# A gated causal convolution without padding columns in its token ring: shorter older taps and one product per run

## The chip, the cores and the metric

The kernel runs on one core of a Trainium2 chip. The metric is device time in microseconds (us) of one execution. Engines in the profile: PE is TensorE's matmuls, PEld its weight loads, DVE is VectorE, ACT is ScalarE, POOL is GpSimd, SP issues nearly all transfers. Times in ns are single instructions.

## The reference

Attention in blocks of 64 over 8 batches, 8 heads, 576 tokens, 64 numbers per head; its output is turned into x (8 x 576 x 512) and goes through a gated layer with a causal depthwise convolution of five taps:

```
scores = q @ k^T / 8, where block(i) >= block(j);   attn = softmax(scores) @ v
x   = attn, heads side by side                        # B x 576 x 512
xp  = 4 zero tokens ahead of each batch of x
gate_pre[s] = sum over k=0..4 of conv_w[k] * xp[s + k] # per channel
out = (sigmoid(gate_pre) * (x @ w_val)) @ w_out
```

Tap k = 4 is the token itself; tap k < 4 is the token 4-k back. A batch's first tokens have no older ones: there the reference reads zeros.

## The kernel before, in words

The whole order of work is written out by hand: PLAN (lines 12 to 116) is a list of words such as `C/1/P/4+5+6+7`, that is step, arguments, engine (P is PE, V DVE, A ACT, G POOL, S SP), PSUM banks. The last lines of the kernel go through it once and call the function of each word; each engine executes its own words in that order and waits only for data and buffers. Eight PSUM banks are shared by all.

**Attention.** `lq`, `lk`, `lv` load on SP; `cd`, `cv` cast to fp16 on POOL or DVE; `Tt` turns q and k on PE and `Te` copies them from PSUM into qkT; `S` computes scores of 128 keys and `E` their exponentials on ACT (pt); `mka`, `mkb` zero masked corners on POOL; `A` multiplies with v, `Nr` and `Nm` divide by the sums on DVE (x16); `X` turns the result on PE, and `Xe` copies it into the ring. The last 64 tokens of a batch go by `SL`, `EL`, `AT`, `NTr`, `NTm`, `XT`, `XTe`. `Sh` and `Eh` are halves of `S` and `E` at the start.

**The token ring.** xt (line 226 on, tile "xt") holds x turned, 128 partitions x 4 channel groups x the tokens of four batches side by side; batch b lies in slot b mod 4. Ahead of each slot, and after the last, lie 4 columns of zeros, which `px` writes once on POOL (lines 335 to 339). So a slot has 580 columns, and the ring 2320 (RING, line 138). `Xe` (line 584) and `XTe` (line 573) write at slot + 4.

**The convolution, the value and the product.** The ring is cut into five runs of 464 columns (RUN); as batches 4 to 7 take the place of 0 to 3, runs 0 to 4 are done a second time as 5 to 9. For run n:

- `C` (line 626): 80 matmuls. Each has a 32x32 diagonal of convolution weights (DG) as its loaded weights and streams 464 columns. For each of five taps it goes over d and over four row groups of 32 partitions (line 633: channel group g = (row + d) mod 4), so that the 16 matmuls of one tap sit on 16 different 32x32 tiles of the array; row decides the PSUM bank, g the 32 output partitions. Tap kk reads the ring at o + kk.
- `CS` (line 639), twice: tanh on ACT of two banks each into th (the sigmoid is 0.5 * (1 + tanh(x/2)); the 0.5 is folded into w_out).
- `V` (line 645), four times: four matmuls of 128x128 weights (w_val) that stream 464 ring columns each.
- `Ve` (line 653), four times: (th + 1) * value on DVE into gv, which has no padding; so it issues one operation for each batch that the run touches, one or two.

`O` (line 673) multiplies 128 tokens of gv with w_out, `Oe` copies to SBUF, `Od` stores. In runs 1, 2 and 3 (and 6, 7, 8) a batch starts inside the run; in 0 and 4 (5 and 9) none does.

Of the kernel before, what the change touches and what calls it, by code (L numbers as in the profile page):

```python
# [26 lines left out]
Nr/0/V A/1/P/2+3 Nm/0/V lwv/1/S E/4.1/A cd/3.1/G S/4.0/P/6+7 Nr/1/V lwv/0/S S/5.2/P/0+1 Nm/1/V  # L27
E/4.0/A lwo/1/S X/0/P/4+5 Tt/3.1/P/4+5 cv/3/G S/4.2/P/2+3 lq/4.1/S Te/3.1/V E/5.2/A mka/3/G
w0/1.128.0/P/6 lq/4.0/S mkb/3/G X/1/P/6+7 mkb/2/G A/3/P/6+7 lk/4.0/S E/4.2/A Xe/0/V lv/4.1/S cv/2/G
S/6.0/P/0+1 Nr/3/V S/5.1/P/4+5 Nm/3/V cvt/0/G E/6.0/A A/2/P/2+3 px//G Xe/1/V mka/4/G X/3/P/2+3  # L30
E/5.1/A S/6.1/P/6+7 mkb/4/G Nr/2/V AT/0/P/0 Nm/2/V E/6.1/A lk/4.1/S Xe/3/V S/5.0/P/4+5 NTr/0/V
X/2/P/2+3 lv/6.0/S w0/1.128.0/P/1 E/5.0/A Xe/2/V mka/6/G S/7.2/P/6+7 NTm/0/V cwv/1/G S/6.2/P/2+3
E/7.2/A C/0/P/0+1+4+5 lv/6.1/S cwv/0/V E/6.2/A cwo/0/V V/0.3/P/6 CS/0.1/A lq/5.0/S cwo/1/G V/0.2/P/7
CS/0.0/A Ve/0.3/V S/7.1/P/4+5 V/0.0/P/2 Ve/0.2/V E/7.1/A lq/5.1/S cd/4.0/G W//P/0+1+6+7 Ve/0.0/V
lv/5.1/S S/7.0/P/4+5 We/1/A We/0/V V/0.1/P/3 lv/5.0/S mkb/6/G cv/4/G lv/7.1/S E/7.0/A Tt/4.0/P/6+7
Ve/0.1/V lv/7.0/S XT/0/P/2 cd/4.1/G A/4/P/0+1 Te/4.0/A lvt/1/S O/0.0/P/3 Nr/4/V Nm/4/V lk/5.0/S
# [83 lines left out]
def kernel(  # L120
# [10 lines left out]
    nc = tc.nc  # L131
    fp32 = mybir.dt.float32
    fp16 = mybir.dt.float16
    AF = mybir.ActivationFunctionType
    ALU = mybir.AluOpType

    B, H, SEQ, D = q.shape
    RING, RUN = 4 * (4 + SEQ), 464
    out2d = out.rearrange("b s n -> (b s) n")

    made = []

    def mm(out, lhsT, rhs, start=True, stop=True):
        made.append(nc.tensor.matmul(out=out, lhsT=lhsT, rhs=rhs, start=start, stop=stop,  # L144
                                     skip_group_check=True))
# [9 lines left out]
    def const(shape, dt, tag):  # L155
        return cpool.tile(shape, dt, tag=tag, name=tag)

    def consts(n, shape, dt, tag):
        return [const(shape, dt, f"{tag}_{i}") for i in range(n)]
# [5 lines left out]
    def one(b):  # L165
        return PS[0:128, b]

    def pick(t, banks):
        a, e = banks
        return t[0:128, a:e + 1:e - a]  # L170

    def both(banks):
        return pick(PS, banks)

    def one16(b):
        return PS16[0:128, b]

    def both16(banks):
        return pick(PS16, banks)
# [3 lines left out]
    def take(*key):  # L183
        taken.append(where.pop(key))
        return taken[-1]
# [12 lines left out]
    def placed(*key):  # L198
        banks, zs = spots.pop(key)
        return take(*key), 256 * zs[0]  # L200
# [5 lines left out]
    w_val_sb = const([128, 4, 512], fp16, "w_val")  # L206
# [3 lines left out]
    DG = const([128, 20, 32], fp16, "DG")  # L210
# [4 lines left out]

    qks = [consts(3, [128, 2, 576], fp32, f"{n}s") for n in "qk"]
    vs = consts(5, [128, 4, 2, 64], fp32, "vs")
    raw = consts(3, [128, 2, 576], fp16, "raw")
    vts = consts(2, [128, 8, 64], fp32, "vts")
    qk16 = [consts(2, [128, 9, 2, 64], fp16, f"{n}16") for n in "qk"]  # L220
    qkT = consts(3, [128, 2, 2, 640], fp16, "qkT")
# [5 lines left out]
    rcts = consts(2, [128, 4, 1], fp32, "rct")  # L227
    x16 = consts(4, [128, 4, 2, 64], fp16, "x16")
    xds = consts(2, [128, 4, 64], fp16, "xd")
    xt = const([128, 4, RING + 4], fp16, "xt")  # L230
    ths = consts(3, [128, 4, RUN], fp32, "th")
    wz = ths[2].rearrange("p f s -> p (f s)")[0:128, 0:256].bitcast(fp16)
    gv = const([128, 16 * SEQ], fp16, "gv")
    w_val_st = gv[0:128, 0:4096].bitcast(fp32).rearrange("p (f n) -> p f n", f=4)
    gv = gv.rearrange("p (f s) -> p f s", f=4)
# [3 lines left out]
    w_out_16 = osb_all[0:128, 2048:3072].bitcast(fp16).rearrange("p (f n) -> p f n", f=4)  # L239

    def slot(b):
        return (4 + SEQ) * (b % 4)

    def rot(tiles, i):
        return tiles[i % len(tiles)]
# [3 lines left out]
    def copy(eng, out, in_):  # L249
        if eng == "A":  # L250
            i = nc.scalar.copy(out=out, in_=in_)  # L251
        else:
            i = (nc.vector if eng == "V" else nc.gpsimd).tensor_copy(out=out, in_=in_)  # L253
        made.append(i)
# [76 lines left out]
    def pv(eng, bank=None):  # L331
        for t in v16s:
            nc.gpsimd.memset(t[0:128, 0:4, 0:2, 64:65], 1.0)

    @op
    def px(eng, bank=None):
        for i in range(4):
            nc.gpsimd.memset(xt[0:128, 0:4, slot(i):slot(i) + 4], 0.0)
        nc.gpsimd.memset(xt[0:128, 0:4, RING:RING + 4], 0.0)

    @op
    def pt(eng, bank=None):
# [228 lines left out]

    @op
    def XTe(b, eng, bank=None):
        copy(eng, xt[0:128, 0:4, slot(b) + 516:slot(b) + 580],
             one16(take("XT", b))[:, 0:256].rearrange("p (g s) -> p g s", g=4))

    @op
# [5 lines left out]
    @op  # L583
    def Xe(p, eng, bank=None):
        b, g = divmod(p, 4)
        bank, o = placed("X", p)
        copy(eng, xt[0:128, g, slot(b) + 4:slot(b) + 516].rearrange("p (i r s) -> p i r s", i=4, r=2),
             both16(bank)[:, :, o:o + 256].rearrange("p r (i s) -> p i r s", i=4))


# [27 lines left out]
    def We(i, eng, bank=None):  # L618
# [3 lines left out]
        else:  # L622
            made.append(nc.vector.tensor_scalar(out=o, in0=r, scalar1=0.5, scalar2=None, op0=ALU.mult))

    @op
    def C(n, eng, bank):
        o = RUN * (n % 5)
        for i in range(2):
            where["C", n, i] = bank[2 * i:2 * i + 2]
        for kk in range(5):  # L630
            for d in range(4):
                for row in range(4):
                    g = (row + d) % 4
                    rs, cs = slice(32 * row, 32 * row + 32), slice(32 * g, 32 * g + 32)
                    mm(one(bank[row])[cs, 0:RUN], DG[rs, 5 * g + kk, 0:32],
                       xt[rs, g, o + kk:o + kk + RUN], start=(kk == 0), stop=(kk == 4))

    @op
    def CS(n, i, eng, bank=None):
        made.append(nc.scalar.activation(  # L640
            out=rot(ths, n)[0:128, 2 * i:2 * i + 2], in_=both(take("C", n, i))[:, :, 0:RUN],
            func=AF.Tanh, bias=0.0, scale=0.5))

    @op
    def V(n, x, eng, bank):
        o = 4 + RUN * (n % 5)
        where["V", n, x] = bank
        for fc in range(4):
            mm(one(bank)[:, 0:RUN], w_val_sb[0:128, fc, 128 * x:128 * x + 128],
               xt[0:128, fc, o:o + RUN], start=(fc == 0), stop=(fc == 3))  # L650

    @op
    def Ve(n, x, eng, bank=None):
        o, r = RUN * (n % 5), one(take("V", n, x))
        for i in range(4):
            a, e = max(o, slot(i)), min(o + RUN, slot(i) + SEQ)
            if a < e:
                made.append(nc.vector.scalar_tensor_tensor(  # L658
                    out=gv[0:128, x, a - 4 * i:e - 4 * i], in0=rot(ths, n)[0:128, x, a - o:e - o],
                    scalar=1.0, in1=r[:, a - o:e - o], op0=ALU.add, op1=ALU.mult))  # L660


    def project(u, t, r, a, e):
# [47 lines left out]
    for word in PLAN.split():  # L711
        name, args, eng, bank = (word.split("/") + [""])[0:4]
        a = [int(i) for i in args.split(".") if i]
# [51 lines left out]
```

## Time and profile before

| what | value |
| --- | --- |
| three timed runs | 176.15, 177.96 (median), 178.81 us |
| the profiled execution's own time | 176.63 us |
| its span in the trace | 174.8 us |
| PE busy | 166.7 us, 95% of the span |
| ACT, DVE, POOL busy | 144.9, 123.8, 71.6 us |
| moved by DMA | 40.38 MB, 231 GB/s on average |
| granted PE clock | 0.997 of full |

The page lists busy time by engine, the span in 40 slices, the chain of work that ended last, and the costliest groups of instructions; each group's row gives line, engine, operation, out<-in, shapes, count, then busy us, mean ns of one, idle time ahead of it. "64x128" is partitions x columns streamed, "32*32" the tile of the array. Busy PE is not PE at its peak, since matmuls are pipelined.

### The profile page before, as it was taken

The numbers are of one execution on the slowest core, as the hardware profiler recorded it, in microseconds if no ns is written. First come the engines' busy times: TensorE is split into PE (matmuls) and PEld (weight loads), VectorE is DVE, ScalarE is ACT, GpSimd is POOL, SyncE is SP. The second block draws the span as 40 slices with busy tenths as digits, with TensorE's granted clock in tenths as the row PEclk, the third lists the DMA queues.
The fourth block names the chain that finished last, engine by engine and source line by source line (L and its number), as shares of the span: only waits on it lengthen the run. The fifth ranks groups of instructions, "written<-read, shape, count | busy, mean of one in ns | idle before, by whom it ended". The sixth has DMA issues, their size and how long they took to land.

```text
span 174.8 us, 8114 instructions
## 1 busy us (share of the span) xinstructions
PE 166.7 (95%) x3498; PEld 100.4 (57%) x3498; DVE 123.8 (71%) x247; ACT 144.9 (83%) x179; POOL 71.6 (41%) x146
## 2 busy tenths in 40 slices
PE   6999899999999997899999999999999999999991
PEld 1556476456656564577546755566656665665540
DVE  2747898888778791999846998976798695545420
ACT  3699999989999999689889679988798878954562
POOL 5122674982552640576533462253646441100000
PEclk9999999999999999999999999999999999999998
DMA  4999999999999999879899989999994031103175
GB/s 139 302 364 290 248 296 391 307 200 281 189 317 272 201 214 362 252 222 308 252 308 198 281 256 260 306 306 242 332 295 124 4 112 72 64 4 120 38 297 210
DMA packets 53694, 40.38 MB, mean 231 GB/s; under 512 B 39701, under 2 KB 39957, under 8 KB 53658
## 3 DMA queue, kind: packets, MB, share of 16 engines
q1 hardware_dynamic: 53514, 39.74, 78.9%
q8 instruction: 27, 0.44, 1.0%
q10 hardware_dynamic: 144, 0.13, 0.2%
q14 instruction: 9, 0.07, 0.2%
HBM read 30.42 MB, written 9.44 MB: 228 GB/s over the span
## 4 chain that ended last, share of the span: by engine, by line
PE 81%; ACT 6%; DVE 5%; issue 4%; DMA 2%; POOL 0%; DVEq 0%; POOLq 0%; ACTq 0%
PE PS L144 72%; PE PS L148 8%; ACT pt L449 3%; DMA ks<-in_k_dram 2%; ACT qkT L251 2%; DVE qkT L253 2%; DVE x L528 1%; DVE gv L658 1%; DVE xt L253 0%; DVE k L253 0%; DVE rc L523 0%; ACT osb L251 0%; POOL pt L499 0%; POOL pt L494 0%; ACT late L251 0%
## 5 line engine op out<-in xcount | busy, mean ns | idle before, releaser
L449 ACT ACTIVATE pt<-PS 128x1024 f16<-128x1024 f32 (+1 forms) x102 | 93.8, 984 | 10.1 <-PE PS L144 8.5
L144 PE MATMUL PS<-qkT 64*128 64x64 f16 (+4 forms) x512 | 40.2, 260 | 0.8 <-DVE qkT L253 0.5
L144 PE MATMUL PS<-w_out,gv 128*128 128x512 f16 (+1 forms) x148 | 35.8, 374 | 0.2 <-DVE x L528 0.2
L144 PE MATMUL PS<-xt,w_val 128*128 128x464 f16 x160 | 35.7, 360 | 0.0
L253 DVE COPY qkT<-PS 128x1152 f16<-128x1152 f16 (+1 forms) x22 | 29.1, 1327 | 7.4 <-PE PS L148 4.1
L658 DVE SCALAR_TENSOR_TENSOR gv<-th,PS 128x112 f16<-128x112 f32 (+4 forms) x64 | 26.2, 449 | 11.4 <-PE PS L144 6.0
L144 PEld LDWEIGHTS <-pt 128*128 128x128 f16 (+1 forms) x960 | 27.9, 102 | 6.2 <-issue 1.5
L144 PE MATMUL PS<-v,pt 128*128 128x65 f16 (+1 forms) x896 | 31.0, 194 | 0.1
L144 PEld LDWEIGHTS <-qkT 64*128 64x128 f16 x512 | 18.0, 97 | 17.9 <-issue 13.6
L640 ACT ACTIVATE th<-PS 128x928 f32<-128x928 f32 x20 | 17.8, 942 | 6.7 <-PE PS L144 6.6
L528 DVE TENSOR_TENSOR x<-PS,rc 128x512 f16<-128x512 f32 x32 | 22.1, 691 | 1.0
L144 PEld LDWEIGHTS <-w_val 128*128 128x128 f16 x160 | 14.0, 98 | 15.2 <-issue 3.6
L499 POOL MEMSET pt<- 64x256 f16 x32 | 10.4, 329 | 28.9 <-ACT pt L449 28.5
L144 PEld LDWEIGHTS <-gv 128*128 128x128 f16 x148 | 12.6, 97 | 13.4 <-issue 2.3
L253 POOL CAST k<-ks 128x1152 f16<-128x1152 f32 x12 | 14.0, 1166 | 12.3 <-DMA ks<-in_k_dram 7.2
L494 POOL MEMSET pt<- 64x256 f16 x32 | 10.2, 322 | 18.4 <-ACT pt L449 15.9
L253 POOL CAST q<-qs 128x1152 f16<-128x1152 f32 x11 | 13.2, 1201 | 10.2 <-DMA qs<-in_q_dram 9.8
L253 POOL CAST v<-vs 128x512 f16<-128x512 f32 x24 | 14.6, 618 | 6.0 <-DMA vs<-in_v_dram 3.9
L253 DVE COPY xt<-PS 128x512 f16<-128x512 f16 (+1 forms) x30 | 11.6, 397 | 4.5 <-ACT th L640 2.3
L251 ACT COPY qkT<-PS 128x1152 f16<-128x1152 f16 (+1 forms) x16 | 14.3, 908 | 0.4 <-PE PS L148 0.3
L251 ACT COPY osb<-PS 128x512 f32<-128x512 f32 x18 | 10.5, 592 | 3.3 <-PE PS L144 3.0
L144 PE MATMUL PS<-xt,DG 32*32 32x464 f16 x800 | 13.1, 358 | 0.1
(57 smaller groups left out, 140.5 us busy)
## 6 DMA issues: line engine op xcount, KB each, us to landing
ks<-in_k_dram SPq DMA_DIRECT2D x32, 288.0 KB, 5.1
qs<-in_q_dram SPq DMA_DIRECT2D x32, 288.0 KB, 5.7
out_dram<-osb SPq DMA_DIRECT2D x35, 256.0 KB, 4.0
vs<-in_v_dram SPq DMA_DIRECT2D x64, 128.0 KB, 4.9
vts<-in_v_dram SPq DMA_DIRECT2D x8, 128.0 KB, 5.7
osb<-in_moe_w_out_dram SPq DMA_DIRECT2D x2, 512.0 KB, 6.1
gv<-in_moe_w_val_dram SPq DMA_DIRECT2D x2, 512.0 KB
out_dram<-late SPq DMA_DIRECT2D x1, 128.0 KB
```

The source lines that it names most:

```text
L144: made.append(nc.tensor.matmul(out=out, lhsT=lhsT, rhs=rhs, start=start, stop=stop, skip_group_check=True))
L148: made.append(nc.tensor.transpose(out=out, in_=in_, identity=identity))
L251: i = nc.scalar.copy(out=out, in_=in_)
L253: i = (nc.vector if eng == "V" else nc.gpsimd).tensor_copy(out=out, in_=in_)
L449: made.append(nc.scalar.activation(out=o, in_=r, func=AF.Exp, bias=0.0, scale=0.125))
L494: nc.gpsimd.memset(rot(pts, p)[64:128, 0:2, 0:1024].rearrange("p h (t s) -> p h t s", t=2)[:, :, :, 0:64], 0.0)
L499: nc.gpsimd.memset(rot(pts, p)[64:128, 0:2, 640:1408].rearrange("p h (t s) -> p h t s", t=2)[:, :, :, 0:64], 0.0)
L528: made.append(nc.vector.tensor_tensor(out=rot(x16, p)[0:128].rearrange("p i h d -> p h i d"), in0=r[:, :, :, 0:64], in1=rot(rcs, p)[0:128] ...
L640: made.append(nc.scalar.activation(out=rot(ths, n)[0:128, 2 * i:2 * i + 2], in_=both(take("C", n, i))[:, :, 0:RUN], func=AF.Tanh, bias=0.0 ...
L658: made.append(nc.vector.scalar_tensor_tensor(out=gv[0:128, x, a - 4 * i:e - 4 * i], in0=rot(ths, n)[0:128, x, a - o:e - o], scalar=1.0, in ...
```

## The change

The ring loses its padding: slots of 576 columns, 2304 in all, and no `px`. The run edges are written out: 0, 460, 920, 1382, 1842, 2304, so runs have 460 or 462 columns. Tap 4 goes first and streams the whole run, opening the sums in its banks. The older taps leave out the first 4-kk tokens of a batch: where a batch starts inside the run, the new function `tap` returns two pieces, one up to the start and one from start + (4-kk) on, and the loop issues the four row groups of the first piece and then those of the second, for each d. With the batch starts at 576, 1152 and 1728, run 1 is cut into 116 and 344 columns, run 2 into 232 and 230, run 3 into 346 and 114 (less the columns left out of the second piece); run 0 has one piece with its start moved. `Ve` issues one operation for a run. All other words of PLAN stay as they are and where they are.

```diff
-    RING, RUN = 4 * (4 + SEQ), 464
+    RING, EDGES = 4 * SEQ, (0, 460, 920, 1382, 1842, 2304)
...
-    xt = const([128, 4, RING + 4], fp16, "xt")
-    ths = consts(3, [128, 4, RUN], fp32, "th")
+    xt = const([128, 4, RING], fp16, "xt")
+    ths = consts(3, [128, 4, 462], fp32, "th")
...
     def slot(b):
-        return (4 + SEQ) * (b % 4)
+        return SEQ * (b % 4)
+
+    def run(n):
+        return EDGES[n % 5], EDGES[n % 5 + 1]
...
-    def px(eng, bank=None):
-        for i in range(4):
-            nc.gpsimd.memset(xt[0:128, 0:4, slot(i):slot(i) + 4], 0.0)
-        nc.gpsimd.memset(xt[0:128, 0:4, RING:RING + 4], 0.0)
...
+    def tap(o, e, back):
+        starts = [s for s in range(0, RING, SEQ) if o <= s < e]
+        cuts = [o] + [s for s in starts if s > o] + [e]
+        return [(a + back * (a in starts), z) for a, z in zip(cuts, cuts[1:])]
...
     def C(n, eng, bank):
-        o = RUN * (n % 5)
+        o, e = run(n)
...
-        for kk in range(5):
+        for kk in (4, 0, 1, 2, 3):
             for d in range(4):
-                for row in range(4):
-                    g = (row + d) % 4
...
-                    mm(one(bank[row])[cs, 0:RUN], DG[rs, 5 * g + kk, 0:32],
-                       xt[rs, g, o + kk:o + kk + RUN], start=(kk == 0), stop=(kk == 4))
+                for a, z in tap(o, e, 4 - kk) if kk < 4 else [(o, e)]:
+                    for row in range(4):
+                        g = (row + d) % 4
...
+                        mm(one(bank[row])[cs, a - o:z - o], DG[rs, 5 * g + kk, 0:32],
+                           xt[rs, g, a + kk - 4:z + kk - 4], start=(kk == 4), stop=(kk == 3))
...
     def Ve(n, x, eng, bank=None):
-        o, r = RUN * (n % 5), one(take("V", n, x))
-        for i in range(4):
-            a, e = max(o, slot(i)), min(o + RUN, slot(i) + SEQ)
-            if a < e:
-                made.append(nc.vector.scalar_tensor_tensor(
-                    out=gv[0:128, x, a - 4 * i:e - 4 * i], in0=rot(ths, n)[0:128, x, a - o:e - o],
-                    scalar=1.0, in1=r[:, a - o:e - o], op0=ALU.add, op1=ALU.mult))
+        o, e = run(n)
+        made.append(nc.vector.scalar_tensor_tensor(
+            out=gv[0:128, x, o:e], in0=rot(ths, n)[0:128, x, 0:e - o], scalar=1.0,
+            in1=one(take("V", n, x))[:, 0:e - o], op0=ALU.add, op1=ALU.mult))
```

## The prediction, made before the changed kernel ran

> **What bounds the kernel now.** I read the page first: busy times, the 40 slices, the chain of work that ended last, and the groups by shape.
>
> ```profile
> PE 166.7 (95%) x3498; PEld 100.4 (57%) x3498; DVE 123.8 (71%) x247; ACT 144.9 (83%) x179; POOL 71.6 (41%) x146
> PE   6999899999999997899999999999999999999991
> DMA  4999999999999999879899989999994031103175
> PE 81%; ACT 6%; DVE 5%; issue 4%; DMA 2%; POOL 0%; DVEq 0%; POOLq 0%; ACTq 0%
> ```
>
> PE is at 9 tenths or more in nearly every slice, and 81% of the chain is PE. The one dent in the middle is at slices 15 and 16 (65 to 75 us). I asked for the waits of PE, the matmuls around the dent, and busy time on both sides of it.
>
> ```profile
> PE PS L148 <- DVE q L253: 1.2, 1, 1.2
> PE PS L144 <- DVE tiny L699: 1.2, 1, 1.2
> PE PS L148 <- DVE k L253: 0.8, 1, 0.8
> PE PS L144 <- DVE qkT L253: 0.5, 1, 0.5
> PE PS L144 <- DVE x L528: 0.2, 1, 0.2
> ...
> 65.58 1.44 PE L144 MATMUL PS<-xt,DG 32*32 32x464 f16 x80
> 66.96 0.40 PE L144 MATMUL PS<-qkT 64*128 64x320 f16 x8
> 67.29 1.74 PE L144 MATMUL PS<-xt,w_val 128*128 128x464 f16 x8
> 70.25 0.44 PE L148 MATMUL PS<-ident,q 64*128 64x64 f16 x18 [1.22 <-DVE q L253]
> ...
> 69.43 0.76 DVE L253 CAST q<-qs 128x1152 f16<-128x1152 f32 x1 [3.71 <-issue]
> 70.10 1.30 DVE L658 SCALAR_TENSOR_TENSOR gv<-th,PS 128x228 f16<-128x228 f32 x4
> ...
> POOL k L253 <- DMA ks<-in_k_dram: 3.7, 1, 3.7
> ...
> 65.00:75.00 10.00, 8.55 (x192) 4.88 (x190) 6.26 (x13) 8.28 (x11) 3.44 (x6) 1.00 0.92 288
> 75.00:174.00 99.00, 96.10 (x2035) 58.09 (x2033) 67.80 (x140) 78.15 (x96) 35.09 (x64) 1.00 0.68 203
> ```
>
> These are all the waits of PE that the profile names, and after the start there are only two: 1.22 us ahead of 70.25, and 0.2. The first is a late load: DVE sat 3.71 us before its cast of q, POOL 3.7 us for a load of k, with the transfers busy. After 75 us PE is busy in 96.10 of 99 us (last columns: DVE, ACT and POOL have room). So whatever lengthens PE's stream before 70 us can hide in 1.22 us of idle time, and after 75 us it is paid in full.
>
> **What the change does to the convolution.** It removes no tap. In runs 1, 2, 3 and 6, 7, 8 four taps of five are issued as two pieces: 16 tiles x 4 taps = 64 more matmuls a run, 384 in all (800 become 1184), each with its own weight load, for the same columns. So I need to know what holds a tap now. First the group and the neighbours by shape, then windows cut through run 1 (only its convolution; columns: stretch, length, PE busy with matmuls in flight, PEld likewise).
>
> ```profile
> L144 PE MATMUL PS<-xt,DG 32*32 32x464 f16 x800 | 13.1, 358 | 0.1
> L144 PE MATMUL PS<-qkT 64*128 64x128 f16 x64 | 8.1, 232 | 0.1
> L144 PE MATMUL PS<-qkT 64*128 64x320 f16 x64 | 11.1, 315 | 0.1
> ...
> 47.73 1.27 PE L144 MATMUL PS<-xt,DG 32*32 32x464 f16 x80
> 48.94 0.44 PE L148 MATMUL PS<-ident,q 64*128 64x64 f16 x18
> ...
> 47.73:47.78 0.06, 0.05 (x16) 0.05 (x16) 0.00 (x0) 1.00 0.09 18
> 47.78:47.94 0.15, 0.15 (x16) 0.14 (x32) 0.00 (x0) 1.00 0.25 91
> 47.94:47.99 0.05, 0.05 (x32) 0.05 (x1) 0.00 (x0) 1.00 1.06 299
> 47.99:48.13 0.14, 0.14 (x32) 0.04 (x1) 0.00 (x0) 1.00 0.72 254
> 48.13:48.25 0.12, 0.12 (x38) 0.12 (x15) 0.00 (x0) 1.00 0.95 353
> ```
>
> The 16 matmuls of a tap start within 0.05 us, all side by side; the next 16 start at 47.94, the third tap at 48.13: 0.20 us a tap, though one matmul lasts 358 ns. Look at the loads: those of tap 2 all ran ahead, during tap 1. Of tap 3 just one did; the other 15 began only at 48.13, 0.40 us after tap 1 began, when its matmuls (358 ns) were through. In between exactly 32 matmuls were in flight. I read this as a limit: about 32 matmuls with their loads, that is 64 instructions, are open at once, and one leaves only when it is through. The Trainium skill, page "TensorE: Matmul & The Clock Gate", gives in its table of specifications an engine queue 64 deep; the row's 32 and 32 agree.
>
> With 32 open and 0.40 us each, two taps of 16 take 0.40 us: the limit and the streaming just meet, which is why it costs nothing now. A cut tap has 32 matmuls and fills it alone. A piece of 232 columns lasts some 0.28 us (between the 232 ns of 128 columns and the 315 of 320, an estimate), plus the 0.04 us that 0.40 is over 358 ns: 0.32 us. That is the least for a cut tap under this limit; the most is 0.40, when the second piece waits for the first and the two last as long as a whole. Now it is 0.20. So 0.12 to 0.20 more a tap; I take 0.15, nearer the short end, because pieces of different tiles overlap. 6 runs x 4 taps = 24 cut taps: 24 x 0.15 = **+3.6 us on PE** (2.9 to 4.8). From outside, the bounds are 0 (each tile simply streams its two pieces; the columns are the same) and the first rival's 6.0.
>
> Of this, runs 1 (47.73) and 2 (65.58) come before the dent: 8 taps x 0.15 = 1.2 us against 1.22 idle. The cast of q waits for a transfer, not for PE, so I take all 1.2 as hidden: **-1.2**. Without that cover it is paid.
>
> **The rest, part by part.**
>
> ```profile
> L144 PE MATMUL PS<-xt,w_val 128*128 128x464 f16 x160 | 35.7, 360 | 0.0
> L658 DVE SCALAR_TENSOR_TENSOR gv<-th,PS 128x464 f16<-128x464 f32 x8 | 5.1, 636 | 2.5 <-PE PS L144 2.0 <-POOL pt L494 0.2 <-ACT th L640 0.2
> L658 DVE SCALAR_TENSOR_TENSOR gv<-th,PS 128x460 f16<-128x460 f32 x8 | 4.8, 630 | 2.8 <-ACT th L640 2.4
> L658 DVE SCALAR_TENSOR_TENSOR gv<-th,PS 128x348 f16<-128x348 f32 x8 | 4.1, 509 | 0.0
> L658 DVE SCALAR_TENSOR_TENSOR gv<-th,PS 128x112 f16<-128x112 f32 x8 | 2.1, 268 | 0.6 <-PE PS L144 0.5
> L338 POOL MEMSET xt<- 128x16 f16 x4 | 0.3, 125 | 0.0
> ```
>
> - Shorter runs: 460 to 462 columns, 460.8 on average. The value: 35.7 x 3.2/464 = 0.25 us; the convolution 13.1 x 3.2/464 = 0.09. **-0.3**, all on PE.
> - One product for a run: 64 operations become 40. A pair of 112 + 348 takes 268 + 509 = 777 ns, a whole one of 460 630: 0.147 us less, 24 times, 3.5 us of DVE's 123.8. PE hardly ever waits for DVE (list above), so most of it buys nothing. Where it may: the chain after the late load, in which four products (70.10, 1.30 us) precede a copy of qkT. Two pairs there: **-0.3**. Bounds 0 and 0.5 (three pairs).
> - The padding memsets: five of about 0.12 us on POOL, 0.6 us, ahead of the first convolution. POOL has 0% of the chain: 0, with a gain of 0.6 as bound.
> - ACT streams 2 x 3.2 columns less in each tanh; nothing.
> - The tap order and unequal runs change no word of the plan; the changed kernel's instruction streams show 384 loads and 384 matmuls more on PE, none moved, and no further wait there. Queued behind a longer `C` are `V` and the attention's matmuls on PE, and the tanh on ACT; DVE's products wait for both, with room.
>
> **The sum.** 3.6 - 1.2 - 0.3 - 0.3 = +1.8 on the profiled execution's 176.63 us (span 174.8): 178.4. That execution is 1.33 us under the median of the three runs (177.96) and 0.48 over the lowest; I add half of 1.33, since a new median falls between: **179.1 us**.
>
> **Rivals.**
>
> 1. Matmuls start in strict order. Then the second piece of tile group d, which waits for the first piece on its own tiles, also holds back group d + 1, and a cut tap takes four times its first piece. At 0.20 us for 464 columns, 116 columns give 0.20, 232 give 0.40, 346 give 0.60. Extra a tap: 0 for run 1 (0.15 by the limit above), 0.20 and 0.40; a ring 4 x (0.15 + 0.20 + 0.40) = 3.0, both 6.0; less 1.2 in the dent, less 0.6: +4.2, **181.5 us**. Against it, from the start of the kernel, where the program's order is two matmuls of 128 and 384 columns and one of 512 (`Sh`), then 18 transposes of k (`Tt`, line 20 and 21 of the plan):
>
> ```profile
> 13.13 0.28 PE L144 MATMUL PS<-qkT 64*128 64x128 f16 x1
> 13.14 0.23 PE L148 MATMUL PS<-ident,k 64*128 64x64 f16 x1
> 13.21 0.95 PE L144 MATMUL PS<-qkT 64*128 64x384 f16 x2
> ```
>
> The first transpose (other row half of the array) began at 13.14, ahead of the 384 and the 512 that stand before it. So order isn't strict across row groups. In the change, though, the blocked piece and the next group share their row groups and differ in columns, and no row here shows passing there. This rival stays likely. The Trainium skill, same page, Part 3, "The mechanism", has matmuls start and end strictly in program order. By that rule the time is this rival's; the trace contradicts it in this one place.
>
> 2. The cut is free: a tile streams its pieces back to back, and the limit of 32 isn't what I take it for. Then only the gains are left: 176.63 - 0.6 + 0.7 = **176.7 us**, not slower than before. It is decided by whether a cut tap takes 0.20 us or over 0.30. For it: the columns are the same and loads run ahead; against: the 15 loads that did not.
>
> 3. The dent hides nothing, since transfers are issued behind stores that wait for PE, and the load comes later by as much: +1.2, **180.3 us**. Against it: the transfers of that stretch are busy (0.92 of all engines in the row of 65 to 75 us), so they hardly wait for issue.
>
> 4. The change doesn't shorten the products: excluded, since 24 operations are gone from DVE's stream.
>
> **Chances.** Forecast 0.43, rival 1 0.27, rival 2 0.15, rival 3 0.12, something faster 0.03. The forecast's own range is 178.0 to 180.4 (its 2.9 to 4.8, DVE's 0 to 0.5). Rival 1 reaches about 1 us over its 181.5. Range for 8 in 10: 176.5 (takes in most of rival 2) to 182.5. Two per cent is about what a measurement tells from no change: under 174.4 or over 181.5. Slower by that: half of rival 1, a little of rival 3 and of the forecast, and the unmodelled: 0.25; faster 0.03; within 0.72.
>
> **What would show it.** Under the forecast the changed runs' convolutions grow from 1.27 us to about 1.9 each, nearly alike for runs 1, 2 and 3; under rival 1 run 3 (346 columns first) grows to 2.9, run 2 to 2.1, run 1 to 1.9; under rival 2 all stay at 1.3. The idle 1.22 us ahead of the transposes at 70 us shrinks to almost nothing (rival 3: stays). L658's group becomes 40 operations of about 632 ns, 25.3 us. The memsets of xt are gone without a trace elsewhere. The forecast is wrong if PE's added time, summed over the six runs, is under 2 or over 5 us, or if new waits of PE appear behind the convolution.

## The result and the profile after

The changed kernel takes 192.44 us, the median of six runs (191.16 to 194.88), against 178.44 for the kernel before beside it (176.15 to 178.89): 1.083 times as long, 95% interval 1.078 to 1.087. The prediction was 179.1, its range 176.5 to 182.5; both are far off. The profiled execution took 192.0 us; its span is 190.2, 15.4 us longer than before. (Two of the experiments below have a median and no ratio, because three of their four runs were disturbed; the undisturbed one took 190.15 us with the sliver and 190.53 us with the shift.)

From the page of the changed kernel come busy times, the slices of PE and of its granted clock, the queue that carries instructions, the chain by engine, and two groups:

```profile
PE 172.8 (91%) x3882; PEld 104.3 (55%) x3882; DVE 122.8 (65%) x223; ACT 144.9 (76%) x179; POOL 70.8 (37%) x141
...
PE   5999898999599997799969999999599999969992
...
PEclk9999999999969999999999999999999999999999
...
q8 instruction: 30, 0.49, 1.1%
...
PE 79%; issue 7%; DMA 5%; ACT 4%; DVE 2%; POOL 1%; SPq 0%; DVEq 0%; ACTq 0%; POOLq 0%
...
L658 DVE SCALAR_TENSOR_TENSOR gv<-th,PS 128x460 f16<-128x460 f32 (+1 forms) x40 | 24.8, 632 | 21.0 <-PE PS L144 11.1
...
L144 PE MATMUL PS<-xt,DG 32*32 32x462 f16 (+20 forms) x1184 | 17.7, 295 | 7.3 <-issue 7.3
```

PE is busy for 172.8 us, only 6.1 more than before; the other 9.3 us are new idle time. The single dent of before has gone, and dents are now scattered over PE's row. The convolution's group has 7.3 us of idle time ahead of it, where it had 0.1, and its releaser is "issue": PE waited for nothing that the profile can name. The waits of PE in the changed kernel (waiter, what it waited for; us in total, times, longest):

```profile
PE PS L144 <- issue: 9.4, 6, 2.6
PE PS L148 <- issue: 1.3, 1, 1.3
PE PS L144 <- DVE tiny L699: 1.2, 1, 1.2
PE PS L148 <- DVE k L255: 0.9, 1, 0.9
PE PS L144 <- DVE qkT L255: 0.5, 1, 0.5
```

The two "issue" rows, 10.7 us, are new. The wait for the late q (1.2) and the one for x (0.2) are gone; 10.7 - 1.4 is the 9.3 of idle time. Three windows of PE's timeline in the changed kernel (start, us, group, count; idle time ahead in brackets) show where the holes lie:

```profile
48.14 1.87 PE L144 MATMUL PS<-xt,DG 32*32 32x460 f16 x134
52.64 0.38 PE L144 MATMUL PS<-xt,DG 32*32 32x343 f16 x10 [2.64 <-issue]
52.96 0.44 PE L148 MATMUL PS<-ident,q 64*128 64x64 f16 x18
...
71.06 0.71 PE L144 MATMUL PS<-xt,DG 32*32 32x462 f16 x34
72.76 1.42 PE L144 MATMUL PS<-xt,DG 32*32 32x232 f16 x110 [0.99 <-issue]
74.11 0.40 PE L144 MATMUL PS<-qkT 64*128 64x320 f16 x8
...
76.11 0.20 PE L148 MATMUL PS<-ident,q 64*128 64x64 f16 x2
77.59 0.41 PE L148 MATMUL PS<-ident,q 64*128 64x64 f16 x16 [1.27 <-issue]
...
132.66 1.88 PE L144 MATMUL PS<-xt,DG 32*32 32x460 f16 x144
134.47 0.78 PE L144 MATMUL PS<-v,pt 128*128 128x65 f16 x20
135.08 0.38 PE L144 MATMUL PS<-w_out,gv 128*128 128x512 f16 x1
137.61 0.81 PE L144 MATMUL PS<-w_out,gv 128*128 128x512 f16 x3 [2.15 <-issue]
```

Run 1's convolution breaks off after 134 of its 144 matmuls, run 2's after 34; another hole splits 18 transposes, and the last splits the four matmuls of an output projection, well behind run 6's convolution. So neither an operation nor its data makes a hole. What the places share is their number. With PE's instructions counted from 0 in order of time (3,882 loads, 3,882 matmuls and ten others, 7,774 in all), the holes stand ahead of numbers 961, 1985, 2753, 3009, 4033, 5825 and 7361, and each of these, divided by 256, leaves 193.

| hole ahead of PE instruction | it lasts, start to start, us | the 256 before it were used up in, us |
| --- | --- | --- |
| 961 (run 0) | 0.88 | 4.72 |
| 1985 (run 1) | 2.94 | 1.54 |
| 2753 (run 2) | 1.24 | 4.38 |
| 3009 (behind run 2) | 1.47 | 3.36 |
| 4033 (runs 3 and 4) | 2.05 | 1.41 |
| 5825 (behind run 6) | 2.53 | 1.99 |
| 7361 (run 8) | 1.64 | 1.81 |

Queue q8, kind "instruction", makes 30 transfers of 16,384 bytes, one for each 256 of PE's 7,774 instructions; before there were 27 for 7,006. In each of the eleven kernels measured here, q8 makes exactly as many transfers as PE crosses such boundaries (27 to 35). In the trace of the changed kernel each hole ends 1.2 to 1.6 us after one of these transfers is through, and that transfer had started only 0.8 to 3.3 us after PE crossed the boundary before. My reading: PE's program is brought in by blocks of 256, one while the block before it is used, and PE, having used up a block faster than another can be brought, stands still. The Trainium skill, page "Runtime: NRT & Kernel Launch", section "Instruction fetch mechanics", says that the instructions of an engine are refilled in 16 KiB blocks of 256, the next one while the current one runs; the numbers agree. It also says that the cost of crossing such a boundary is mostly hidden; in this kernel it is not.

The 15.4 us then divide so. Gaps of over 0.1 us at these boundaries sum to 12.75 us after and 1.20 before: +11.5. The cut convolutions, from first start to the next operation and without their holes, are longer by 0.67 (run 1), 0.44 (2), 0.48 (3 with 4), 0.58 (6), 0.58 (7) and 0.65 (8): +3.4. The granted clock fell once, soon after the longest hole, as the windows of the changed kernel show (stretch, length, PE, PEld, DVE, ACT, POOL busy, granted clock):

```profile
54.00:58.00 4.00, 4.00 (x34) 1.52 (x34) 2.12 (x3) 2.65 (x3) 0.00 (x0) 0.57 1.01 280
58.00:62.00 4.00, 4.00 (x76) 2.41 (x77) 3.47 (x8) 3.85 (x5) 0.96 (x3) 1.00 1.17 209
```

0.57 over 4 us is 1.7 us of PE's time lost. Less the 1.4 of waits that went and the 0.3 that I had put on shorter runs (not measured alone), that makes 14.9 of 15.4.

### The profile page after: what moved, and what is told of

It is laid out like the page before. It is cut to its first block, busy times and chain, and to the rows that moved or that the text cites. A ratio compares the mean times of both kernels' runs of the same rounds, so it can differ in the third digit from the quotient of the medians.

```text
span 190.2 us, 8853 instructions
## 1 busy us (share of the span) xinstructions
PE 172.8 (91%) x3882; PEld 104.3 (55%) x3882; DVE 122.8 (65%) x223; ACT 144.9 (76%) x179; POOL 70.8 (37%) x141
## 4 chain that ended last, share of the span: by engine, by line
PE 79%; issue 7%; DMA 5%; ACT 4%; DVE 2%; POOL 1%; SPq 0%; DVEq 0%; ACTq 0%; POOLq 0%
PE PS L144 71%; PE PS L148 8%; DMA ks<-in_k_dram 5%; ACT pt L445 3%; ACT qkT L253 1%; DVE qkT L255 1%; POOL k L255 1%; DVE xt L255 0%; DVE k L255 0%; DVE x L524 0%; ACT osb L253 0%; SPq L683 0%; DVE rc L519 0%; ACT late L253 0%; ACTq L445 0%
## 5 line engine op out<-in xcount | busy, mean ns | idle before, releaser
L658 DVE SCALAR_TENSOR_TENSOR gv<-th,PS 128x460 f16<-128x460 f32 (+1 forms) x40 | 24.8, 632 | 21.0 <-PE PS L144 11.1
L144 PE MATMUL PS<-xt,w_val 128*128 128x460 f16 (+1 forms) x160 | 36.5, 365 | 0.0
L643 ACT ACTIVATE th<-PS 128x920 f32<-128x920 f32 (+1 forms) x20 | 17.7, 937 | 18.4 <-PE PS L144 18.3
L144 PE MATMUL PS<-xt,DG 32*32 32x462 f16 (+20 forms) x1184 | 17.7, 295 | 7.3 <-issue 7.3
L144 PEld LDWEIGHTS <-gv 128*128 128x128 f16 x148 | 12.7, 97 | 15.4 <-issue 4.3
L144 PEld LDWEIGHTS <-DG 32*32 32x32 f16 x1184 | 13.1, 88 | 11.6 <-issue 10.1
L255 POOL CAST v<-vs 128x512 f16<-128x512 f32 x24 | 15.1, 640 | 6.5 <-DMA vs<-in_v_dram 4.8
L255 POOL CAST q<-qs 128x1152 f16<-128x1152 f32 x11 | 12.7, 1154 | 11.0 <-ACT pt L445 5.8
```

The costliest lines, as they stand in the source:

```text
L643: made.append(nc.scalar.activation(out=rot(ths, n)[0:128, 2 * i:2 * i + 2, 0:e - o], in_=both(take("C", n, i))[:, :, 0:e - o], func=AF.Tan ...
L658: made.append(nc.vector.scalar_tensor_tensor(out=gv[0:128, x, o:e], in0=rot(ths, n)[0:128, x, 0:e - o], scalar=1.0, in1=one(take("V", n, x ...
```

## The experiments

Theory A: the cut doubles the number of PE instructions in a convolution, and the supply of instructions can't follow. Rival B: the ring or the single product has disturbed something. Rival C: a cut tap is slow in itself, because pieces wait for each other in strict order.

**The change without its cut.** Older taps stream the whole run; all else is as in the changed kernel. This kernel leaves out the boundary: the first four tokens of a batch that starts inside a run also take tokens of the batch ahead of it.

```diff
-                for a, z in tap(o, e, 4 - kk) if kk < 4 else [(o, e)]:
+                for a, z in [(o + (4 - kk) * (o == 0), e)]:
```

> The changed kernel with its older taps in one piece again (the 384 additional matmuls and loads are gone; the first 4 tokens of a batch that starts inside a run take the tokens of the batch before, so part of the output is left wrong). Ring without padding and one product per run stay. Theory A, code loading: PE's instructions arrive in blocks of 256, and a block takes 3.5 to 5.6 us to arrive after the one before it was begun; cut convolutions use a block up in 1.4 to 2.0 us and PE then stands still. Without cuts the seven large holes of PE (1.2 to 2.9 us each) go, and the cut taps' own 3.4 us: about 176 to 178 us, near the kernel before. Rival B, the ring or the single product: the layout of the ring or the later product delays work; then over 185 us stays.

Measured: 177.99 us (ten runs) against 178.3, ratio 0.9985 (0.994 to 1.004). The waits of PE in this kernel:

```profile
PE PS L144 <- issue: 0.9, 2, 0.5
...
PE PS L148 <- DVE q L255: 0.4, 1, 0.4
```

Without the cut the loss is gone, and "issue" is down from 10.7 us to 0.9. The ring and the single product together are worth nothing that can be measured, and rival B falls.

**The cut without the change.** The kernel before, padded ring and all; four taps of five are issued as two pieces, cut at the batch's start.

```diff
+        at = (0, 116, 232, 348, 0)[n % 5]
...
+                for a, z in [(0, at), (at, RUN)] if at and kk else [(0, RUN)]:
...
-                    mm(one(bank[row])[cs, 0:RUN], DG[rs, 5 * g + kk, 0:32],
-                       xt[rs, g, o + kk:o + kk + RUN], start=(kk == 0), stop=(kk == 4))
+                        mm(one(bank[row])[cs, a:z], DG[rs, 5 * g + kk, 0:32],
+                           xt[rs, g, o + kk + a:o + kk + z], start=(kk == 0), stop=(kk == 4))
```

> The kernel before, whole, with its padded ring and its two products per run; only four of five taps of runs 1, 2, 3 (and 6, 7, 8) are cut in two pieces at the batch start, as in the change: 384 more matmuls with their loads. Theory A (code loading): as slow as the changed kernel, 189 to 194 us, with holes of 1 to 3 us in PE wherever the 256-instruction boundary comes within about 4 us of the one before it, all at the same place modulo 256 (number 193). Rival B (ring or product): within 2% of before, at most 182 us (3.4 us for the cut taps).

Measured: 191.78 us, ratio 1.082 (1.074 to 1.089), the whole loss of the change. The waits of PE in this kernel:

```profile
PE PS L144 <- issue: 8.5, 5, 3.3
PE PS L148 <- issue: 1.8, 1, 1.8
```

The holes stand ahead of the same instruction numbers as in the changed kernel, but for 2753. The cut alone is the cause; what it does beside adding instructions, the next two ask.

**A sliver cut off.** As the last, but the pieces are 8 and 456 columns in all six runs, so that hardly any streaming is divided, and the number of instructions is the same.

```diff
+        at = (0, 8, 8, 8, 0)[n % 5]
```

> As the run with the padded ring and cut taps, but each cut tap goes in pieces of 8 and 456 columns in all six runs: the same 384 additional instruction pairs, and a first piece that is through at once. Theory A (code loading): the number of instructions decides, not the pieces: 188 to 194 us, holes as before. Rival C (strict order, a cut tap takes four times its first piece): four times 8 columns is nothing, so 176 to 179 us. By the limit of 32 open matmuls alone (my prediction's step, 0.15 us a cut tap): 179 to 182 us.

Measured: 193.77 us, median of four (190.15 to 197.33), no ratio. PE's timeline around run 1 in this kernel:

```profile
48.01 1.93 PE L144 MATMUL PS<-xt,DG 32*32 32x464 f16 x134
52.50 0.60 PE L144 MATMUL PS<-xt,DG 32*32 32x456 f16 x10 [2.56 <-issue]
```

The same break after the same 134 matmuls. Without holes its convolutions last 1.96 us (runs 6 and 7), no less than the same runs in the changed kernel (1.81 and 1.78). How the columns are shared out doesn't matter, the number of instructions does; rival C, which gave 176 to 179, falls, and so do the 179 to 182 of the limit of 32 open matmuls by itself.

**Half of the cuts.** The padded ring, only two taps cut: 192 more matmuls in place of 384.

```diff
-                for a, z in [(0, at), (at, RUN)] if at and kk else [(0, RUN)]:
+                for a, z in [(0, at), (at, RUN)] if at and kk > 2 else [(0, RUN)]:
```

> The kernel before with its padded ring, cut as in the change but in two taps of five instead of four: 192 more matmuls instead of 384. Cut taps by themselves (0.15 us each, 12 of them): +1.8 us. Theory A: a block that a convolution of 224 instructions falls into lasts about 2.3 us instead of 1.5 and the hole after it is shorter by that, 1 to 2 us, where the boundaries come to lie badly: in all 183 to 188 us, between before and the change. Rival (cut work alone): 180 us.

Measured: 185.15 us, ratio 1.046 (1.042 to 1.050), some half of the loss. Gaps at the boundaries sum to 7.6 us, between 1.2 and 12.1 (all four taps). Dose and effect go together.

**Bursts of tiny matmuls.** To measure a block by itself, the kernel before got 512 matmuls of four columns, each with its load, ahead of run 6's convolution, and 512 more at the very end, where few transfers run. Their results aren't used.

```diff
+            mm(one(bank[row])[cs, 0:4], DG[rs, 0, 0:32], DG[rs, 0, 0:4])
...
-C/6/P/0+1+6+7
+bu/512/P/0+1+6+7 C/6/P/0+1+6+7
```

> The disputed cost by itself: the kernel before, with 512 additional tiny matmuls of 4 columns (1024 instructions with their loads, over all 16 tiles, their results overwritten or unused) put ahead of the convolution of run 6 (at about 122 us, where transfers are busy) and 512 more at the end of the program (where they are idle). Theory A (code loading): within a burst PE runs in steps of 256 instructions: 1 to 2 us of work, then a hole up to the next block, 3.4 to 5.6 us from boundary to boundary in the middle, and less, perhaps 2.5 to 3.5 us, at the end, if busy transfers are what makes a block late. Rival (the holes come from the cut pieces or from what the convolution waits for): the bursts run through at 8 to 30 ns a pair, 4 to 15 us in one piece.

Measured: 204.6 us in one run. PE's timeline in this kernel, in the burst and at the end:

```profile
123.62 0.94 PE L144 MATMUL PS<-DG 32*32 32x4 f16 x101
125.38 1.16 PE L144 MATMUL PS<-DG 32*32 32x4 f16 x128 [0.83 <-issue]
130.21 1.17 PE L144 MATMUL PS<-DG 32*32 32x4 f16 x128 [3.67 <-issue]
135.31 1.17 PE L144 MATMUL PS<-DG 32*32 32x4 f16 x128 [3.93 <-issue]
139.03 0.28 PE L144 MATMUL PS<-DG 32*32 32x4 f16 x27 [2.56 <-issue]
...
189.51 1.59 PE L144 MATMUL PS<-DG 32*32 32x4 f16 x179
193.94 1.18 PE L144 MATMUL PS<-DG 32*32 32x4 f16 x128 [2.84 <-issue]
197.67 1.17 PE L144 MATMUL PS<-DG 32*32 32x4 f16 x128 [2.55 <-issue]
201.12 0.75 PE L144 MATMUL PS<-DG 32*32 32x4 f16 x77 [2.28 <-issue]
```

This is the mechanism bare: 128 pairs, that is 256 instructions, in some 1.1 us, then a hole, and again. From one resumption to the next it takes 4.8, 5.1 and 3.7 us in the middle, 3.7 and 3.5 at the end. A block thus costs 3.5 to 5.1 us, 14 to 20 ns per instruction, however little work it holds; at the quiet end that is at the top of what I had expected or a little over. Of these times 1.05 to 2.4 us pass between the boundary and the start of the next transfer on q8, and 2.4 to 3.0 us from there until PE goes on; the first part differs most. A cut convolution uses its 288 instructions in 1.8 us, 6 ns each.

**The changed kernel, its blocks shifted.** 64 tiny pairs at the start move every boundary by 128 instructions.

```diff
-lq/0.0/S w0/2.128.0/P/0
+lq/0.0/S w0/2.128.0/P/0 sh/64/P/0
```

> The changed kernel with 64 tiny matmuls of 4 columns (128 instructions) added at the very start of PE's stream, where PE waits for the first load anyway, so that every later instruction stands 128 further. Theory A: the holes stay at number 193 modulo 256 and so move by 128 instructions in the program; run 1's convolution (288 instructions) is now shared by two blocks about half and half, so its one hole of 2.9 us becomes two of 1 to 2 us, and the other holes change likewise; in total 7 to 14 us of holes, 187 to 194 us. Rival (holes are tied to the pieces): they stay at the same matmuls and sizes, 192 us.

Measured: 193.62 us, median of four (190.53 to 195.17), no ratio. The holes keep their remainder of 193 and fall on other matmuls: PE's timeline in this kernel, run 1 and what follows:

```profile
54.70 1.09 PE L144 MATMUL PS<-xt,DG 32*32 32x460 f16 x70
56.53 1.08 PE L144 MATMUL PS<-xt,DG 32*32 32x341 f16 x74 [0.73 <-issue]
...
61.63 0.48 PE L144 MATMUL PS<-qkT 64*128 64x64 f16 x10 [0.29 <-issue]
```

Run 1's hole of 2.94 us has become two, 1.03 and 0.59 from start to start, the first of them 64 matmuls earlier in the convolution, since 128 instructions are 64 pairs. Run 0's uncut convolution has a hole of 2.79 us that it didn't have. Gaps at the boundaries sum to 11.5 us, within the 7 to 14 expected. The place follows the count of instructions, not the operation.

**The kernel before, its blocks shifted.** The same 64 pairs, without the change, as a control.

> The kernel before with the same 128 tiny instructions at the start. Theory A: its blocks last 4.6 us and more, close above a load's 3.4 to 5.6 us, so a shift moves which blocks are short: within 2% of before either way, its own hole of 0.4 us (run 0's convolution, instruction 961) gone or moved, others of up to 1 us possible. Rival (the shift costs or gains by itself): more than 2%.

Measured: 185.95 us, ratio 1.052 (1.049 to 1.055). That is a miss: I expected no difference. PE's timeline in this kernel around run 0:

```profile
33.22 1.39 PE L144 MATMUL PS<-xt,DG 32*32 32x464 f16 x79
37.59 0.36 PE L144 MATMUL PS<-xt,DG 32*32 32x464 f16 x1 [2.98 <-issue]
```

A whole uncut convolution, 160 instructions in 1.2 us, now lay in one block with 96 other short instructions; the block was used up in 2.87 us, and PE stood still. Its gaps sum to 7.6 us against 1.2. Beside that the granted clock was at 0.50 from 11 to 24 us, after the tiny matmuls, and again from 38 to 41, after this hole. Run 0's convolution starts 2.7 us later than in the kernel before (33.22 against 30.56 us), run 1's 7.2 later (54.94 against 47.73), and run 9's 9.7. The 4.5 us between the first two are, to 0.1 us, this hole (3.33 us from start to start in place of the 0.44 before) and 1.7 us of lowered clock; of the 2.7 us ahead of run 0, 1.0 us is a hole ahead of 961, and the rest wasn't separated. So the kernel before isn't free of the limit; its short instructions happen to fall well against the boundaries.

**One product per run, alone.** The padded kernel with a padded gv, so that one operation serves a run; where 128 tokens span two batches, the product with w_out loads 64 columns twice (32 more PE instructions).

```diff
-        for i in range(4):
-            a, e = max(o, slot(i)), min(o + RUN, slot(i) + SEQ)
...
+        made.append(nc.vector.scalar_tensor_tensor(
+            out=gv[0:128, x, o:o + RUN], in0=rot(ths, n)[0:128, x, 0:RUN],
```

> The other half alone: the kernel before with one product per run on the padded ring (gv keeps the padding columns; the product with w_out of the 128 tokens across a batch start takes two loads of 64, 32 more matmuls in all), 24 fewer operations on DVE. The prediction's step (0.3 us gained behind the late load, no more, since PE waits for DVE nowhere else): 0 to 0.5 us faster, ratio 0.997 to 1.000. Rival: DVE counts for more than its waits show: 1.5 us or more gained (ratio under 0.992). A loss of up to 0.5 us would be the 32 matmuls or a block boundary that they move.

Measured: 179.57 us, ratio 1.011 (1.003 to 1.019): about 1% slower, where I expected the same or a gain, another miss. The waits of PE in this kernel:

```profile
PE PS L144 <- issue: 1.2, 1, 1.2
...
PE PS L144 <- ACT pt L449: 1.0, 1, 1.0
```

Gaps at the boundaries sum to 2.8 us against 1.2, behind blocks of 4.7 and 4.6 us. But the larger one, 1.59 us ahead of 961, comes before any PE instruction that this edit adds, and the hole there is between 0.44 and 1.66 us in the nine kernels that have the same count of instructions up to it: it varies that much by itself. The wait of 1.0 us for ACT is new too. What costs the 1% isn't shown. The 3.5 us of DVE's time bought nothing that can be seen.

**The same instructions, spread out.** If a block needs its 3.5 to 5 us whatever it holds, long matmuls among the short ones must shrink the holes. In the changed kernel, each cut convolution of runs 1, 2, 7 and 8 got two groups of the value that used to follow it between its taps, and run 6's one output projection. PE's order alone changes.

```diff
-C/1/P/4+5+6+7
+Ct/1.0/P/4+5+6+7 Ct/1.1/P/4+5+6+7 V/1.2/P/0 Ct/1.2/P/4+5+6+7 Ct/1.3/P/4+5+6+7 V/1.0/P/1 Ct/1.4/P/4+5+6+7
```

> The changed kernel with the same instructions in another order on PE: two groups of the value (8 matmuls of 460 columns, some 1.8 us) go between the taps of the cut convolutions of runs 1, 2, 7 and 8, ahead of tap 3 and ahead of the last, and one output projection (about 1 us) ahead of the third tap of run 6. No other engine's order changes. Theory A (a block of 256 needs 3.5 to 5 us, whatever it holds): a hole shrinks by the time of the long matmuls that now lie in its block. Run 1's 2.94 us should fall to about 1.2, run 6's 2.53 to about 1.5, run 8's 1.64 to nearly nothing; run 2's two holes (1.24 ahead of its first long group, 1.47 with such groups in its block already) and run 3's 2.05 stay. That is 4.4 us less, and up to 1.7 more where the granted clock no longer falls behind run 1: 186 to 188.5 us. Rival (the added instructions cost their time wherever they stand): 191 to 193, holes as they were. Rival (banks that are wanted earlier turn the holes into waits for ACT and DVE): holes shrink as said, new waits of PE for ACT or DVE of the same size, 190 to 193.

Measured: 195.53 us, ratio 1.098 (1.079 to 1.116), no better than the change. The waits of PE in this kernel (its plan stands on one line, so line numbers are about 100 lower: L42 and L46 issue matmuls and transposes, L546 is the tanh, L343 the exponential):

```profile
PE PS L42 <- issue: 4.5, 4, 2.0
PE PS L46 <- ACT th L546: 2.8, 2, 1.6
PE PS L42 <- ACT th L546: 2.2, 3, 1.2
...
PE PS L42 <- ACT pt L343: 0.8, 1, 0.8
```

And PE's timeline of this kernel from run 1's convolution on:

```profile
51.06 0.94 PE L42 MATMUL PS<-xt,DG 32*32 32x116 f16 x64
51.94 0.95 PE L42 MATMUL PS<-xt,w_val 128*128 128x460 f16 x4
52.82 0.46 PE L42 MATMUL PS<-xt,DG 32*32 32x116 f16 x32
53.21 0.44 PE L46 MATMUL PS<-ident,q 64*128 64x64 f16 x18
54.42 0.40 PE L42 MATMUL PS<-qkT 64*128 64x128 f16 x4 [0.77 <-ACT th L546]
```

The holes went as theory A said, and further: run 1's 2.94 us and both of run 2's are gone, run 6's is 1.34 instead of 2.53, run 8's 0.38 instead of 1.64, run 3's, not spread, stays at 2.38. All gaps at boundaries sum to 5.9 us in place of 12.75, with every instruction still there. That decides for the density of instructions. But the time isn't theory A's 186 to 188.5: the last of the rivals came with it, and by the median cost more than its 190 to 193. The convolution now ends later by the groups put into it, the tanh that reads its banks comes later too, and PE waits 6.6 us for ACT (5.0 for the tanh, the rest for exponentials and a copy), which it didn't do in the changed kernel; "issue" is 6.2 us less. My reading is that the holes had also given ACT its time. PE is busy for 172.8 us, as in the changed kernel, though its clock doesn't fall here; where those 1.7 us went wasn't looked into.

## Why the prediction was wrong, point by point

- **The step that failed** is the last of "the rest, part by part": the changed kernel's streams show 384 loads and 384 matmuls more on PE, "and no further wait there". I priced the added instructions by the array's time alone and their supply at nothing. The runs showed a wait of its own: +11.5 us of holes, and 1.7 of lowered clock behind one of them. Put into my sum of +1.8, they make +15.0 on 176.63, 191.6 us; the execution took 192.0.
- **The cut tap's own cost** was right: 0.15 us a tap, 3.6 in all; 3.4 measured. That run 1 and run 8 (116 and 346 columns first) grow alike, by 0.67 and 0.65, fits the limit of 32 open matmuls. That this limit is the reason wasn't tried by itself.
- **Rival 1** wanted 2.9 us for the convolution with 346 columns first; run 8 took 1.86 without its hole. **Rival 2** wanted 1.3 for all. Both fall. The Trainium skill's rule of strict order, weighed there, doesn't show here either.
- **The dent**: the 1.22 us of waiting for q are gone (rival 3 wanted them to stay). But the holes ahead of it alone would have covered them: PE came to these transposes at 76.11 us instead of 70.25, when q had long been cast (at 71.86). That the dent hides a small delay, as I said, is shown by the kernel without the cut: its run 2 starts 0.98 us later than before, its wait for q is 0.43 us instead of 1.22, and its transposes start at 70.37 us, only 0.12 later.
- **The products** are as foreseen, 40 of 632 ns (24.8 us). The 0.6 us that I had put on them and on shorter runs would be a ratio of 0.997, within the interval of the kernel without the cut (0.994 to 1.004): neither shown nor refuted.
- **The forecast's own range** is mis-added: by its terms it goes from 178.2 (0.7 and 0.2 less) to 180.6 (1.2 and 0.3 more), not from 178.0 to 180.4. Nothing hangs on it.
- **The forecast's own sign of error** did appear: new waits of PE behind the convolution.

The clue stood in the profile of before. Two rows of its page and its timeline, not read for this:

```profile
q8 instruction: 27, 0.44, 1.0%
```

```profile
30.56 1.78 PE L144 MATMUL PS<-xt,DG 32*32 32x464 f16 x80
```

27 transfers of 16 KB for 7,006 instructions is one for each 256. Run 0's convolution took 1.78 us where the same 80 matmuls of run 1 took 1.27; inside it lies a gap of 0.44 us, ahead of instruction 961, after a block used up in 4.7 us. So the kernel before already stood at the edge with blocks of 4.7 us, and a cut convolution of 288 instructions at some 1.9 us (1.27 + 4 x 0.15, my own figures) fills more than a block. By 4.7 us a block that is a hole of about 2.8 us for each of six runs: some 17 us, an estimate that takes every block to be as slow as that one. 11.5 us came: blocks took from 3.5 to 5.6 us, and run 7's convolution fell across a boundary so that neither of its blocks ran dry.

What stays open: why a transfer of instructions starts 1.05 us after a boundary in one place and 2.4 in another, so that a block takes 3.5 us or 5.1 (the one at the quiet end, the other with transfers busy, which fits but wasn't varied alone); the rest of the first 2.7 us in the shifted kernel before; what makes the single product 1% slower by itself; and the 0.5 us that my division leaves over. No version ran that beats the kernel before: without the cut it is equal, and that is about as much as a cheaper cut could give.

## What to carry to other kernels

Count an engine's instructions against time, not only against work: here every block of 256 that PE used up in less than 3.2 us was paid with a hole, and some of those that lasted 3.3 to 5.2 us were, so that splitting matmuls cost more than three times what the pieces cost the array (11.5 against 3.4 us). Here an "issue" wait whose places share a remainder modulo 256 in PE's instruction count was supply, not data; fewer instructions cured it. Spreading them among long ones shrank it too, but that pays only where what waits for the last of them can bear the delay. And look in the profile of before for the small instance of a cost, here the gap of 0.44 us, before pricing the large one at nothing.

## What the runs showed of the hardware

- PE's instructions come by 256: boundaries at the same remainder in all kernels here; 3.5 to 5.1 us for a block in the bursts, and from 3.5 to 5.6 us from one boundary to the end of the next hole in the changed kernel. A shift by 128 instructions alone cost the kernel before 5%.
- The granted clock fell to 0.50 for 3.41 us behind some holes and not behind others: behind 2.94 us in the changed kernel, 2.08 and 3.64 in the padded one with cuts, but not behind 2.53 in the changed kernel nor 3.02 in the sliver's. In each trace its changes lie on a grid of 3.41 us. Leaving out the first 30 us, the end of the program and the bursts, there were seven falls in all kernels, each at the end of a grid interval in which PE stood idle for 1.77 to 3.16 us; intervals that no fall followed had at most 1.82. So the place of a hole counts beside its length: of the changed kernel's hole of 2.94 us, 2.07 of idle time lay in one interval, of that of 2.53 us only 1.70. The Trainium skill, page "TensorE: Matmul & The Clock Gate", Part 1, has a free-running window of about 3.4 us decide on the clock by PE's activity; the grid agrees. It puts the lower clock after an idle window of about 3.4 us; here 1.8 to 2 us of idle time within one were enough.
- A tap of 32 pairs on 32x32 tiles costs 0.11 to 0.17 us more than one of 16 with the same columns, whether the first piece has 116, 232 or 346 of them, and 0.19 with a first piece of 8.
